# A fused retention and two-MoE-layer kernel: raw weights staged up to four tiles ahead, sixteen weight splits moved from VectorE to GpSimd, and half sums held in four buffers

## The chip, the cores and the metric

The kernel runs on one core of one Trainium2 chip. The metric is the device time of one execution in microseconds (us), lower is better. The core's engines are TensorE (PE in the rows, with its weight loads as PEld), VectorE (DVE), ScalarE (ACT), GpSimd (POOL) and SyncE (SP). Every transfer in this kernel is issued by SyncE's queue, in the order in which the program records it.

## The reference, cut to what matters

```python
# attention without softmax: B=4, H=8, S=768, D=64, one decay gamma per head
state = gamma * state + k[t] (x) v[t];   y[t] = scale * q[t] @ state
x = y as 3072 tokens x 512
# first layer, d_ff = 2048
h = x @ w_in;  g = h * sigmoid(1.702 * h);  x = g @ w_out
# second layer, d_ff = 1536
out = (sigmoid(x @ w_gate) * (x @ w_val)) @ w_out
```

All inputs are float32 except that the weights of both layers come to the kernel as 64-bit words (the bit patterns of doubles), which it converts itself.

## The kernel before, in words

**Arithmetic.** Each float32 operand of a large matmul is split into a rounded high part and a remainder (`wh`, `wl` for weights, `xh`, `xl` for tokens, `gh`, `gl` for the activation), and each product is three matmuls: high by high, high by low, low by high. ScalarE makes the high part, and VectorE or GpSimd subtracts to get the low part (`split_w`, lines 262 to 267, for a 128x512 weight tile).

**First phase, up to about 735 us of the profile.** The tokens are six blocks of 512 (`b` from 0 to 5), the first layer's inner dimension is sixteen slices of 128 (`f`). One pair `(b, f)` is a unit, 96 in all. A unit projects (`proj`, lines 270 to 275, twelve matmuls into a bank `h`), applies the gate (ScalarE L279, VectorE L280, ScalarE L283, VectorE L288), and two units later adds its output product (`emit_out`, lines 364 to 366, twelve matmuls into the four banks `acc`). The units run in segments: slices 0 to 7 of block 0, slices 0 to 7 of block 1, slices 8 to 15 of block 0, slices 8 to 15 of block 1, then blocks 2 to 5 with all sixteen slices each. So units 0 to 7 are the first segment, 8 to 15 the second, 16 to 23 the third, 24 to 31 the fourth. At the end of a segment `emit_out` moves the four banks to SBUF (tiles `ost`, two buffers) and stores them: as half sums to a DRAM tensor `halfd` after the first two segments, as the finished block to `x2d` after the others. In the third and fourth segment the half sums come back (`load_half`, three tiles at the segment's start and the fourth at its end) and are added.

Attention for the next block is cut into pieces (scores, state update, result) and one or two pieces are recorded with each unit. Their inputs `in_t` come through SyncE's queue into six buffers (`load_next`).

**Weights.** 68 tiles have to be converted: first 32 of the first layer, whose result stays in SBUF as `wraw`, then 36 of the second, whose result goes to a DRAM tensor `w2d`. `stage` (lines 202 to 208) issues the load of a raw tile (512 KB) into one of four buffers `w64` (named `w` in the rows). `convert` (lines 210 to 260) returns four steps that the unit's code calls at different points: a scaling on ScalarE (L228), two bit operations on VectorE (L233, L236), two more (L242, L246), and the sum (L256), on GpSimd for the first layer and on VectorE for the second, where the store to `w2d` (L258) follows. The last reader of a raw buffer is L246. Each of units 0 to 7 converts two tiles, units 8 to 20 one tile each, which ends the first layer's, and then five units of each eight convert a second-layer tile. The staging before keeps two raw tiles (units 0 to 6) or one (later) loaded ahead.

**What orders the work.** The schedule is manual: each engine runs its instructions in the order in which the loop over the units records them, and waits at the head of its queue. In a unit the order is: scaling and upper bits of this unit's conversion; the twelve `proj` matmuls; the split of the next unit's projection weight (`split_for`); the gate; the split of an output weight (`split_out`, always on GpSimd); lower bits; an attention piece; `gl`; the conversion's sum (and store); `stage`; perhaps a second attention piece; the output product of two units ago.

```python
            conv[3]()
            stage((2 if i < FH - 1 else 1) - len(staged))
            if items and b < 2:
                items.popleft()()
            pend.append(i)
            while pend and i - pend[0] >= DEPTH:
                emit_out(pend.popleft())
```

**Second phase, from about 735 us to the end.** The second layer runs as 36 chains of block products (lines 748 to 791). The change touches no line of it.

Of the kernel before, what the change touches and what calls it, by code (L numbers as in the profile page):

```python
# [8 lines left out]
F32 = mybir.dt.float32  # L9
# [6 lines left out]
P = 128  # L16
# [8 lines left out]
def retention_moe_moe2(  # L25
# [12 lines left out]
    nc = tc.nc  # L38
# [12 lines left out]
    def pool(stack, name, bufs, side, **kw):  # L51
        return stack.enter_context(tc.tile_pool(name=name, bufs=bufs, side=side, reuse_waits="tile", **kw))
# [5 lines left out]
    g_p = pool(left, "g", 2, "left")  # L58
# [3 lines left out]
    in_p = pool(right, "inp", 6, "right")  # L62
# [6 lines left out]
    def psum_tile(kind, shape=(P, 512)):  # L69
        i = turn[kind][0]  # L70
        turn[kind].rotate(-1)
        return psum[i].tile(list(shape), F32, name=kind, tag="bank")
# [11 lines left out]
    halfd = [dram.tile([P, KC, 512], F32, name=f"half{i}") for i in range(2)]  # L84
# [109 lines left out]
    raw1 = {}  # L194
    staged = deque()
# [6 lines left out]
    def stage(n=1):  # L202

        for _ in range(min(n, len(to_stage))):
            ph, f, k = to_stage.popleft()
            t = cv_p.tile([P, 512], U64, name="w64", tag="w64", bufs=4)
            nc.sync.dma_start(out=t, in_=(w1 if ph == "1" else w2)[f, k])
            staged.append((ph, f, k, t))
# [53 lines left out]
    def split_w(raw, lo_engine):  # L262
        wh = wsp_p.tile([P, 512], F32R, name="wh", tag="wh")
        wl = wsp_p.tile([P, 512], F32R, name="wl", tag="wl")
        nc.scalar.copy(wh, raw)  # L265
        lo_engine.tensor_tensor(out=wl, in0=raw, in1=wh, op=ALU.subtract)  # L266
        return wh, wl
# [22 lines left out]
    x_t, w_t, g_t, acc_t, half_t = {}, {}, {}, {}, {}  # L290
# [4 lines left out]
    def att_items(j):  # L295

        t0, n = blocks1[j]
        items = []
        for i in range(n // C):
            s = t0 // C + i  # L300

            def first(s=s, i=i):
                if i == 0:
                    alloc_x(j)
                emit_scores(s)
                if s >= 3:
                    load_next(s + 1, KN, V)

            def second(s=s):
                emit_update(s)  # L310
                if s >= 3:
                    load_next(s + 2, Q, K)

            def third(s=s, i=i):
                if s + 1 < NSTEP:
                    emit_prep(s + 1)
                emit_y(s, *x_t[j], i * C)

            items += [first, second, third]
        return deque(items)  # L320
# [3 lines left out]
    FH = F1 // 2  # L324
# [7 lines left out]
    def split_out(i):  # L332

        j = i - DEPTH
        if 0 <= j < len(units):
            w_t[j, "out"] = split_w(raw1[units[j][1], 1], nc.gpsimd)

    def split_for(i):

        if i < len(units):  # L340
            b, f = units[i]
            w_t[i, 0] = split_w(raw1[f, 0], nc.gpsimd if i < FH else nc.vector)

    def load_half(b):
        t = in_p.tile([P, 512], F32, name="half", tag="half", bufs=3)
        nc.sync.dma_start(out=t, in_=halfd[b][:, len(half_t[b]), :])
        half_t[b].append(t)

    def emit_out(i):
        b, f = units[i]  # L350
        if (b, f) in starts:
            acc_t[b] = [psum_tile("acc") for _ in range(4)]
            if f:
                half_t[b] = []
                for _ in range(3):
                    load_half(b)
        acc = acc_t[b]
        _, gh, gl = g_t.pop(i)
        wh, wl = w_t.pop((i, "out"))
        n = blocks1[b][1]  # L360
        st, sp = (b, f) in starts, (b, f) in ends
        for c in range(4):
            a, wc = acc[c][:, :n], slice(c * P, (c + 1) * P)
            nc.tensor.matmul(a, wh[:, wc], gh[:, :n], start=st, stop=False)  # L364
            nc.tensor.matmul(a, wl[:, wc], gh[:, :n], start=False, stop=False)  # L365
            nc.tensor.matmul(a, wh[:, wc], gl[:, :n], start=False, stop=sp)  # L366
        if not sp:
            return
        for c in range(4):
            t = g_p.tile([P, 512], F32, name="ost", tag="ost")  # L370
            if b in half_t:
                nc.vector.tensor_tensor(out=t, in0=acc[c], in1=half_t[b][c], op=ALU.add)
                if c == 0:
                    load_half(b)
            elif c % 2:
                nc.scalar.copy(t, acc[c])
            else:
                nc.vector.tensor_copy(t, acc[c])  # L378
            nc.sync.dma_start(out=(x2d if f == F1 - 1 else halfd)[b][:, c, :], in_=t)
# [20 lines left out]
    def open_early():  # L400
        p2["x"] = pool(ctx, "x2", 1, "right")
        p2["xt"] = pool(ctx, "xt", 6, "right")
        p2["w"] = [pool(ctx, "we", 1, "right")]
# [13 lines left out]
    def prep_x(g):  # L417

        hl = [
            [p2["x"].tile([P, 2, 512], F32R, name=f"{n}{j}", tag=f"{n}{j}") for n in ("xoh", "xol")] for j in range(7)  # L420
        ]
        xo[g] = hl
        for k in range(2):
            raw = {}
            for j, half, kk in ((B11, 0, k), (B12, 1, k), (B22, 1, k + 2), (B21, 0, k + 2)):
                raw[j] = p2["xt"].tile([P, 512], F32, name="xt", tag="xt")
                nc.sync.dma_start(out=raw[j], in_=x2d[2 * g + half][:, kk, :])
            yield
            for j in (T1, T2):
                raw[j] = p2["xt"].tile([P, 512], F32, name="xt", tag="xt")  # L430

            def diff(j, a, b):
                nc.gpsimd.tensor_tensor(out=raw[j], in0=raw[a], in1=raw[b], op=ALU.subtract)

            def split(j, engine):
                h, l = hl[j]
                nc.scalar.copy(h[:, k, :], raw[j])
                engine.tensor_tensor(out=l[:, k, :], in0=raw[j], in1=h[:, k, :], op=ALU.subtract)

            diff(T1, B12, B11)  # L440
            split(B11, nc.vector)
            yield
            diff(T2, B22, T1)
            split(B21, nc.vector)
            yield
            raw[T3] = raw[B12]
            diff(T3, B12, B22)
            split(T2, nc.vector)
            yield
            raw[T4] = raw[B21]  # L450
            diff(T4, B21, T2)
            split(T1, nc.vector)
            yield
            split(T3, nc.vector)
            yield
            split(T4, nc.gpsimd)
            split(B22, nc.vector)
            yield
# [174 lines left out]
    with tc.manual_schedule():  # L633
# [54 lines left out]
        for i, (b, f) in enumerate(units):  # L688
            if i == 0:
                items = att_items(1)  # L690
            elif (b, f) == (1, FH):
                items = att_items(2)
            elif b > 1 and f == 0:
                items = att_items(b + 1) if b + 1 < len(blocks1) else deque()
                if b == len(blocks1) - 1:
                    assert not staged and not to_stage
                    right.close()
                    open_early()
                    xs = prep_x(0)
                    load_chain(0)  # L700
            first = staged and staged[0][0] == "1"
            conv = [lambda: None] * 4
            if first:
                conv = convert(2 if i < FH else 1, nc.gpsimd)
            elif staged and (5 * i) // 8 > (5 * (i - 1)) // 8:
                conv = convert(1, nc.vector)
            xh, xl = x_t[b]
            n = blocks1[b][1]
            conv[0]()
            conv[1]()  # L710
            hb = psum_tile("h")
            proj(hb, w_t.pop((i, 0)), xh, xl, n)
            if i > 0:
                split_for(i + 1)
            g_t[i] = gated(hb, n)
            split_out(i + 1)
            conv[2]()
            if items and (b < 2 or f >= 1):
                items.popleft()()
            gated_lo(g_t[i], n)  # L720
            conv[3]()
            stage((2 if i < FH - 1 else 1) - len(staged))
            if items and b < 2:
                items.popleft()()
            pend.append(i)
            while pend and i - pend[0] >= DEPTH:
                emit_out(pend.popleft())
            next(xs, None)
            if b == len(blocks1) - 1:
                if f == 9:  # L730
                    sums(0)
                elif f in (11, 13):
                    split_chain(0, f == 13)()
# [141 lines left out]
```

## Time and profile before

| | |
|---|---|
| time, median of 3 runs | 1310.52 us (1307.9 to 1313.17) |
| the profiled execution's own time | 1308.13 us |
| its span | 1306.3 us |
| TensorE busy | 1218.8 us, 93% of the span |
| VectorE busy | 802.1 us, 61% |
| ScalarE busy | 546.3 us, 42% |
| GpSimd busy | 523.5 us, 40% |
| mean granted TensorE clock | 0.982 |

About 1.8 us of the profiled execution's time lie outside the span. Busy times are unions of an engine's instructions. A TensorE record covers a matmul from start to its modelled end, so records overlap: the distance between two starts tells the pace, and idle time counts from the end of the last record.

### The profile page before, as it was taken

What the parts mean: (1) busy time and instruction counts of PE and PEld (TensorE: products, weight loads), DVE (VectorE), ACT (ScalarE), POOL (GpSimd) and SP (SyncE); (2) the same over time, 40 slices, a digit from 0 to 9 for tenths busy, and PEclk for the clock granted to TensorE, in tenths of its full rate; (3) what the DMA queues carried; (4) which work ended last, traced back from release to release, by engine and by line L of the source; (5) the groups of instructions that cost most, each with busy time, mean ns of one, the idle gap of its engine ahead of it and who ended that gap; (6) DMA issues with size and microseconds to landing.
All of it is one profiled execution on the core that took longest, in us unless ns stands there. A gap on an engine that the chain in (4) does not pass through costs nothing.

```text
span 1306.3 us, 16095 instructions
## 1 busy us (share of the span) xinstructions
PE 1218.8 (93%) x5948; PEld 964.9 (74%) x5948; DVE 802.1 (61%) x1073; ACT 546.3 (42%) x964; POOL 523.5 (40%) x390
## 2 busy tenths in 40 slices
PE   7887998998999999989999899999899999899998
PEld 6665766776777777768788678787778777687877
DVE  5988986665666665756577263646554555635454
ACT  5333443343433443434455343435444344535251
POOL 4775442422231322322246362525652535643330
PEclk8889999999999999999999999999999999999999
DMA  8452322534224332332200220203321214211111
GB/s 283 162 192 83 127 105 78 189 109 158 91 103 135 108 127 83 129 105 74 93 28 1 98 80 25 73 25 107 119 73 34 64 44 126 97 57 49 49 33 65
DMA packets 62430, 123.48 MB, mean 95 GB/s; under 512 B 6800, under 2 KB 16016, under 8 KB 62352
## 3 DMA queue, kind: packets, MB, share of 16 engines
q1 hardware_dynamic: 62352, 122.46, 28.6%
q8 instruction: 47, 0.77, 0.3%
q14 instruction: 31, 0.25, 0.1%
HBM read 98.31 MB, written 24.12 MB: 94 GB/s over the span
## 4 chain that ended last, share of the span: by engine, by line
PE 51%; DVE 15%; DMA 9%; issue 8%; ACT 5%; POOL 3%; SPq 1%; ACTq 0%; POOLq 0%; DVEq 0%
PE pa L498 14%; DMA w<-in_w_dram 7%; PE pd L498 5%; PE po L616 4%; PE po L615 4%; PE po L614 4%; PE h L275 3%; PE pb L498 3%; PE h L273 3%; PE h L274 3%; PE acc L364 2%; PE acc L365 2%; PE acc L366 2%; DVE cva L256 2%; DVE sg L280 2%
## 5 line engine op out<-in xcount | busy, mean ns | idle before, releaser
L266 POOL TENSOR_TENSOR wl<-wraw,wh 128x512 fp32r<-128x512 f32 x104 | 150.7, 1449 | 428.8 <-ACT wh L265 401.6
L273 PE MATMUL h<-xh,wh 128*128 128x512 f32 x384 | 157.1, 409 | 26.8 <-ACT wh L265 19.1
L275 PE MATMUL h<-xh,wl 128*128 128x512 f32 x384 | 157.6, 410 | 10.4 <-DVE wl L266 9.3
L365 PE MATMUL acc<-gh,wl 128*128 128x512 f32 x384 | 153.5, 400 | 8.9 <-POOL wl L266 8.9
L364 PE MATMUL acc<-gh,wh 128*128 128x512 f32 x384 | 156.6, 408 | 3.6 <-DVE ost L378 2.8
L274 PE MATMUL h<-xl,wh 128*128 128x512 f32 x384 | 155.1, 404 | 0.2 <-DVE xl L190 0.2
L366 PE MATMUL acc<-gl,wh 128*128 128x512 f32 x384 | 150.5, 392 | 0.0
L498 PE MATMUL pa<-xoh,oh 128*128 128x512 f32 x288 | 115.1, 400 | 16.4 <-ACT u L557 11.7
L490 POOL TENSOR_TENSOR ol<-raw,oh 128x768 fp32r<-128x768 f32 x36 | 66.8, 1857 | 153.1 <-ACT oh L487 152.9
L283 ACT CAST gh<-sg 128x512 fp32r<-128x512 f32 x96 | 59.6, 621 | 160.9 <-DVE sg L280 160.9
L233 DVE TENSOR_SCALAR cva<-cva 128x512 uint32<-128x512 uint32 x68 | 53.8, 795 | 115.0 <-ACT cva L228 114.0
L265 ACT CAST wh<-wraw 128x512 fp32r<-128x512 f32 x192 | 116.2, 613 | 0.2
L498 PE MATMUL pa<-xol,oh 128*128 128x512 f32 x288 | 114.4, 397 | 0.0
L498 PE MATMUL pa<-xoh,ol 128*128 128x512 f32 x288 | 113.3, 393 | 0.8 <-DVE ol L490 0.8
L614 PE MATMUL po<-woh,g2h 128*128 128x512 f32 x288 | 112.4, 390 | 1.1 <-DVE ost L507 1.1
L616 PE MATMUL po<-woh,g2l 128*128 128x512 f32 x288 | 112.5, 391 | 0.0
L615 PE MATMUL po<-wol,g2h 128*128 128x512 f32 x288 | 112.5, 391 | 0.0
L273 PEld LDWEIGHTS h<-xh,wh 128*128 128x128 f32 x384 | 74.6, 194 | 49.9 <-ACT wh L265 26.2
L228 ACT ACTIVATE cva<-w 128x512 f32<-128x512 f32 x68 | 45.4, 669 | 156.2 <-DMA w<-in_w_dram 142.7
L275 PEld LDWEIGHTS h<-xh,wl 128*128 128x128 f32 x384 | 74.6, 194 | 35.1 <-DVE wl L266 17.4
L365 PEld LDWEIGHTS acc<-gh,wl 128*128 128x128 f32 x384 | 72.5, 189 | 30.8 <-POOL wl L266 17.7
L364 PEld LDWEIGHTS acc<-gh,wh 128*128 128x128 f32 x384 | 72.4, 188 | 26.9 <-DVE ost L378 3.6
(108 smaller groups left out, 2521.7 us busy)
## 6 DMA issues: line engine op xcount, KB each, us to landing
w<-in_w_dram SPq DMA_DIRECT2D x68, 512.0 KB, 4.0
in_t<-in_qkv_dram SPq DMA_DIRECT2D x96, 256.0 KB, 3.5
raw<-w2d SPq DMA_DIRECT2D x72, 256.0 KB, 3.1
w2d<-cva SPq DMA_DIRECT2D x36, 256.0 KB, 2.2
wor<-w2d SPq DMA_DIRECT2D x36, 256.0 KB, 2.7
x2d<-ost SPq DMA_DIRECT2D x24, 256.0 KB, 2.9
xt<-x2d SPq DMA_DIRECT2D x24, 256.0 KB, 4.4
out_dram<-ost SPq DMA_DIRECT2D x24, 256.0 KB, 2.0
```

The lines of the kernel that those rows point to most:

```text
L265: nc.scalar.copy(wh, raw)
L266: lo_engine.tensor_tensor(out=wl, in0=raw, in1=wh, op=ALU.subtract)
L273: nc.tensor.matmul(bank[:, :n], wh[:, k, :], xh[:, k, :n], start=(k == 0), stop=False)
L274: nc.tensor.matmul(bank[:, :n], wh[:, k, :], xl[:, k, :n], start=False, stop=False)
L275: nc.tensor.matmul(bank[:, :n], wl[:, k, :], xh[:, k, :n], start=False, stop=(k == KC - 1))
L364: nc.tensor.matmul(a, wh[:, wc], gh[:, :n], start=st, stop=False)
L365: nc.tensor.matmul(a, wl[:, wc], gh[:, :n], start=False, stop=False)
L366: nc.tensor.matmul(a, wh[:, wc], gl[:, :n], start=False, stop=sp)
L498: nc.tensor.matmul(bank, w[:, kk], x[:, k, :], start=start and k == 0 and w is wh and x is xh, stop=stop and k == 1 and w is wl, skip_grou ...
L614: nc.tensor.matmul(bank, gh, wh, start=f == 0, stop=False)
L615: nc.tensor.matmul(bank, gh, wl, start=False, stop=False)
L616: nc.tensor.matmul(bank, gl, wh, start=False, stop=f == FR - 1)
```

## The change

Three things are changed in the first phase. `stage` is called so that four raw tiles are loaded or on their way after each unit, with the same four buffers. The low part of the projection weight's split is computed by GpSimd for units 0 to 23, where it was GpSimd for units 0 to 7 and VectorE from unit 8. And for blocks 0 and 1 the four output tiles of a segment's end are four different buffers (three tiles `half` and one `ost`), the half sums are reloaded into the same four at the segment's start, and the sum is written in place. Blocks 2 to 5 use `ost` with two buffers as they did.

```diff
-            w_t[i, 0] = split_w(raw1[f, 0], nc.gpsimd if i < FH else nc.vector)
-
-    def load_half(b):
-        t = in_p.tile([P, 512], F32, name="half", tag="half", bufs=3)
-        nc.sync.dma_start(out=t, in_=halfd[b][:, len(half_t[b]), :])
-        half_t[b].append(t)
+            w_t[i, 0] = split_w(raw1[f, 0], nc.gpsimd if i < 3 * FH else nc.vector)
+
+    def half_tile(c):
+        if c < 3:
+            return in_p.tile([P, 512], F32, name="half", tag="half", bufs=3)
+        return g_p.tile([P, 512], F32, name="ost", tag="ost")
 
     def emit_out(i):
         b, f = units[i]
...
             if f:
                 half_t[b] = []
-                for _ in range(3):
-                    load_half(b)
+                for c in range(4):
+                    half_t[b].append(half_tile(c))
+                    nc.sync.dma_start(out=half_t[b][c], in_=halfd[b][:, c, :])
...
         for c in range(4):
-            t = g_p.tile([P, 512], F32, name="ost", tag="ost")
+            t = half_t[b][c] if b in half_t else half_tile(c) if b < 2 else half_tile(3)
             if b in half_t:
                 nc.vector.tensor_tensor(out=t, in0=acc[c], in1=half_t[b][c], op=ALU.add)
-                if c == 0:
-                    load_half(b)
...
             conv[3]()
-            stage((2 if i < FH - 1 else 1) - len(staged))
+            stage(4 - len(staged))
```

The queue of SyncE where the first second-layer tiles are stored (units 18 to 24; `w_` with a number is one raw tile's buffer as the program names it, so the numbers differ between the programs). Before:

```order
L207 DMA w_1673<-in_w_dram 128x512
L346 DMA half<-half_128 128x512 x3
L207 DMA w_1734<-in_w_dram 128x512
L207 DMA w_1785<-in_w_dram 128x512
L258 DMA w2d<-cva 128x512
L207 DMA w_1836<-in_w_dram 128x512
L258 DMA w2d<-cva 128x512
L207 DMA w_1927<-in_w_dram 128x512
```

Of the change:

```order
L207 DMA w_1679<-in_w_dram 128x512
L357 DMA half<-half_128 128x512 x3
L357 DMA ost<-half_128 128x512
L207 DMA w_1742<-in_w_dram 128x512
L207 DMA w_1793<-in_w_dram 128x512
L258 DMA w2d<-cva 128x512
L207 DMA w_1844<-in_w_dram 128x512
L258 DMA w2d<-cva 128x512
L207 DMA w_1935<-in_w_dram 128x512
```

The pattern is the same, one load behind each store, but the loads are of later tiles. Before, 33 raw tiles stand ahead of the first store, and that store is of the 33rd tile, so the load behind it is of the very next tile to be converted. Now 36 stand ahead of it, and the load behind it is of the tile that is converted fourth from there.

GpSimd's queue in units 7 to 9 (`wl` is a weight's low part, `wraw` a converted first-layer tile). Before:

```order
L266 TENSOR_TENSOR wl<-wraw,wh 128x512
L256 TENSOR_TENSOR wraw<-cva,cvb 128x512 x2
L266 TENSOR_TENSOR wl<-wraw,wh 128x512
L256 TENSOR_TENSOR wraw<-cva,cvb 128x512
L266 TENSOR_TENSOR wl<-wraw,wh 128x512
```

Of the change:

```order
L266 TENSOR_TENSOR wl<-wraw,wh 128x512 x2
L256 TENSOR_TENSOR wraw<-cva,cvb 128x512 x2
L266 TENSOR_TENSOR wl<-wraw,wh 128x512 x2
L256 TENSOR_TENSOR wraw<-cva,cvb 128x512
L266 TENSOR_TENSOR wl<-wraw,wh 128x512 x2
```

A unit had one split and one or two sums on GpSimd, and now has two splits beside them; VectorE's queue has one L266 fewer in each of these units.

## Rows read from the trace of the kernel before

**Rows 1.** Windows: length, busy PE, PEld, DVE, ACT, POOL, granted clock, DMA share, GB/s.

```profile
30.00:112.00 82.00, 64.93 (x391) 50.09 (x387) 74.82 (x99) 34.07 (x63) 55.53 (x37) 0.92 0.48 156
112.00:205.00 93.00, 85.11 (x343) 62.76 (x344) 82.06 (x104) 40.89 (x73) 44.29 (x30) 1.00 0.29 99
205.00:330.00 125.00, 112.69 (x663) 88.67 (x662) 80.50 (x121) 46.89 (x88) 34.20 (x24) 0.97 0.43 138
330.00:640.00 310.00, 289.11 (x1570) 225.84 (x1569) 195.72 (x290) 124.71 (x229) 84.21 (x61) 0.98 0.32 107
```

**Rows 2.** TensorE's waits, 330 to 640 us: total us, times, longest.

```profile
PE h L273 <- ACT wh L265: 13.6, 9, 2.5
PE h L275 <- DVE wl L266: 5.5, 10, 0.6
PE acc L365 <- POOL wl L266: 1.7, 3, 0.6
```

**Rows 3.** TensorE's waits, 205 to 330 us.

```profile
PE h L273 <- ACT wh L265: 5.4, 2, 2.8
PE h L273 <- DVE sg L280: 3.5, 1, 3.5
```

**Rows 4.** Timeline of all engines, around unit 53: start, duration, idle before and releaser.

```profile
439.08 0.33 SPq L258 DMA_DIRECT2D w2d<-cva  x1
...
439.46 0.42 SPq L207 DMA_DIRECT2D w<-in_w_dram  x1
...
443.25 0.66 ACT L228 ACTIVATE cva<-w 128x512 f32<-128x512 f32 x1 [6.72 <-DMA w<-in_w_dram]
...
443.94 0.43 DVE L233 TENSOR_SCALAR cva<-cva 128x512 uint32<-128x512 uint32 x1 [4.89 <-ACT cva L228]
...
444.40 0.69 DVE L236 SCALAR_TENSOR_TENSOR cva<-w,cva 128x512 uint32<-128x512 uint32 x1
```

**Rows 5.** Timeline of TensorE around 410 us.

```profile
409.53 0.39 PE L273 MATMUL h<-xh,wh 128*128 128x512 f32 x1
409.76 0.39 PE L274 MATMUL h<-xl,wh 128*128 128x512 f32 x1
...
410.37 0.63 PE L273 MATMUL h<-xh,wh 128*128 128x512 f32 x1
```

**Rows 6.** Timeline of VectorE, one unit of the second segment.

```profile
145.12 1.31 DVE L233 TENSOR_SCALAR cva<-cva 128x512 uint32<-128x512 uint32 x1
146.47 1.66 DVE L236 SCALAR_TENSOR_TENSOR cva<-w,cva 128x512 uint32<-128x512 uint32 x1
148.05 0.68 DVE L266 TENSOR_TENSOR wl<-wraw,wh 128x512 fp32r<-128x512 f32 x1
148.65 0.68 DVE L280 TENSOR_TENSOR sg<-h,sg 128x512 f32<-128x512 f32 x1
...
151.11 1.31 DVE L233 TENSOR_SCALAR cva<-cva 128x512 uint32<-128x512 uint32 x1
```

**Rows 7.** Timeline of GpSimd, the same unit.

```profile
144.59 1.56 POOL L266 TENSOR_TENSOR wl<-wraw,wh 128x512 fp32r<-128x512 f32 x1 [3.00 <-ACT wh L265]
146.11 1.47 POOL L256 TENSOR_TENSOR wraw<-cva,cvb 128x512 f32<-128x512 f32 x1
```

**Rows 8.** Timeline of ScalarE around the second segment's end.

```profile
169.90 0.60 ACT L279 ACTIVATE sg<-h 128x512 f32<-128x512 f32 x1 [0.31 <-PE h L275]
...
178.88 0.59 ACT L376 COPY ost<-acc 128x512 f32<-128x512 f32 x1 [3.90 <-DMA half<-ost]
...
190.98 0.60 ACT L279 ACTIVATE sg<-h 128x512 f32<-128x512 f32 x1 [0.31 <-PE h L275]
```

**Rows 9.** Waits of ScalarE, VectorE and SyncE's queue, 30 to 112 us.

```profile
ACT cva L228 <- DMA w<-in_w_dram: 8.7, 5, 2.8
...
DVE cva L233 <- ACT cva L228: 6.8, 8, 1.9
...
SPq L207 <- DVE cvb L246: 23.0, 3, 7.8
```

## The prediction

> **What bounds the kernel now.** I read the first phase by stages [rows 1], since the change touches nothing behind about 735 us. VectorE is the fullest engine up to 205 us: it is busy 74.82 of 82 us from 30 to 112 us and 82.06 of 93 us from 112 to 205 us. From 205 us on it falls to 80.50 of 125 and 195.72 of 310 us, and TensorE is the bound, but with holes: it is idle 125 - 112.69 = 12.3 us there and 310 - 289.11 = 20.9 us behind. So three stages have three different limits, and each part of the change falls in another.
>
> What makes the holes behind 330 us is read from TensorE's waits: 13.6 us for ScalarE's `wh`, 5.5 us for VectorE's `wl` right behind it, 1.7 us for GpSimd's `wl` [rows 2]. These add up to 20.8 of the 20.9 us. Unit 53 shows what ScalarE itself was late for [rows 4]. The queue of SyncE takes the store of a converted tile at 439.08 us, when VectorE's sum is done, and only then the load behind it, at 439.46 us. The tile of that load is the one ScalarE wants next, and L228 starts at 443.25 us after 6.72 us of waiting. The cast of the next unit's weight stands behind L228 on ScalarE, so TensorE, which has two units of work in hand, runs dry soon after. This hurts where two units in a row convert, which the rule of five in eight makes happen twice in eight units: the load has one unit's time minus the conversion's own length, and a lone conversion has two.
>
> **Part 1, raw tiles four ahead.** In the queue of the change the load behind a store is of the tile that is converted fourth from there, at least six units later, against a load that needs about 4 us (439.46 to 443.25) [rows 4]. So these waits should all go. The load has to wait for the last reader L246 of its own buffer, but the store ahead of it waits for the sum L256, which comes after L246, so behind 205 us nothing new is waited for.
>
> The sum for 205 to 640 us: idle time that hangs on these waits is 20.8 us [rows 2] and 5.4 + 3.5 = 8.9 us [rows 3] (the 3.5 us stand behind a VectorE that waited for the same load), together 29.7 us in 9 + 10 + 3 + 2 + 1 = 25 holes. A record lasts 0.39 us while the next start normally follows after 0.23 [rows 5], so each hole hides 0.16 us more: 4 us. Third, the clock. Around 410 us, after a hole, a record of the same matmul is 0.63 us long instead of 0.39 [rows 5], which is 0.24 us more, as much again as the pace of 0.23: the lower of the two levels (1.2 instead of 2.4 GHz). The granted clock of 0.98 over 310 us and 0.97 over 125 us [rows 1] lacks at most 0.02 x 310 + 0.03 x 125 = 10 us of full pace, part of it inside the holes; I take 6 us. Sum 29.7 + 4 + 6 = 40 us. I keep 3 us back for holes that another engine opens once this one is closed, since VectorE's busy share will rise from 63% to about 70% there: **37 us**, between 20 (half of it lost again) and 40.
>
> From 30 to 112 us ScalarE waits 8.7 us for raw tiles, and VectorE, the bound there, waits 6.8 us in all for ScalarE's L228 [rows 9]. Not all of these eight waits follow a late load (ScalarE has other reasons to be late with L228, a scaling buffer above all), and the change leaves those. The gain is between 0 and 6.8 us; I take the middle: **3 us**.
>
> **Part 2, sixteen splits to GpSimd.** This falls in units 8 to 23, where VectorE repeats a tight loop of 151.11 - 145.12 = 6.0 us [rows 6], while 24 matmuls at 0.23 us want 5.5. The removed L266 costs 0.60 us of the loop (148.05 to 148.65), which alone would bring 6.0 to 5.4 and leave TensorE as the bound: 14 units x 0.5 = 7 us gained. But the loop shows a price for GpSimd's work. L233 takes 1.31 and L236 1.66 us beside GpSimd's two operations [rows 6, 7], and 0.43 and 0.69 us in a place where GpSimd is idle [rows 4]: 1.85 us lost to two operations, so 0.93 each. A third operation on GpSimd in every unit would, at the same price, cost 0.93 and bring 0.60: the loop becomes 6.3, and 14 x 0.33 = 5 us are lost. What decides is whether the third one lies beside L280, which keeps its 0.68 us when it reads the bank in PSUM, or beside the SBUF operations. GpSimd would be busy some 4.5 of 6 us, too much to miss them all. I take **0 us**, between 7 gained and 5 lost.
>
> The Trainium skill has a rule that speaks against this part (SBUF — State Buffer, "Who interferes with whom"): VectorE instructions with two SBUF inputs or in a two-port mode and GpSimd instructions share a port pair that one holds for its whole instruction while the other is blocked. The slow L233 and L236 agree with it, and so does L280. Were no overlap at all possible, the loop would be GpSimd's three operations plus VectorE's own SBUF work, which the rival below prices; the row of 6.0 us is shorter than the same reckoning for two operations (3.0 + 3.5 = 6.5), so the trace bears it out only in part.
>
> **Part 3, four buffers for half sums.** At the second segment's end ScalarE waits 3.90 us until a store has landed and frees an `ost` buffer, and three units take 190.98 - 169.90 = 21.1 us instead of 18.0 [rows 8]: 3.1 us. With four buffers the four evictions need no store. The moves themselves stay (two on VectorE, about 1.2 us of a full loop, are in the 3.1 and don't go). So some 2 us at each of the first two ends: **4 us**. The ends of the third and fourth segment lie behind 205 us, where TensorE has slack for them; I count nothing for them. Reloading the halves all at the start puts one more transfer into SyncE's queue eight units ahead of its use.
>
> **The sum.** 37 + 3 + 0 + 4 = 44 us off the profiled execution's 1308.1 us, which lies 2.4 us under the median of the runs: about **1265 us**.
>
> **The rivals.** (a) *Another engine takes the place of the load.* With L228 on time, VectorE in two converting units in a row has its conversion twice beside an attention piece, and a late L266 stops TensorE as a late `wh` did. Against it: 63% busy from 330 to 640 us [rows 1], and TensorE's slack of two units. It would halve part 1, 37 / 2 = 18: 1265 + 18 = 1283 us. (b) *GpSimd blocks VectorE in units 8 to 23.* With no overlap the loop is three GpSimd operations (4.5 us) plus VectorE's SBUF work free of disturbance, which is the loop less the loss, L266 and L280 (6.0 - 1.85 - 0.60 - 0.68 = 2.9 us): 7.4 us, which is 14 x 1.4 = 20 us lost: 1285 us. For it: L236 at 1.66 us. Against it: the reckoning that is too long for the loop of before. (c) *Slower than before: the loads stop SyncE's queue in the first segment.* In units 0 to 6 a load now has to wait for L246 of its own unit at the head of the queue, and attention's `in_t` stand behind it. Such waits are there already, 23.0 us in three places, longest 7.8 [rows 9]. If each of 7 units stopped TensorE's attention for 7.8 us, 55 us would be lost against 41 gained elsewhere: 1322 us. It decides from about 6 us per unit; but `in_t` is loaded a step or more ahead, and the queue already spends such time waiting without TensorE waiting for a transfer. (d) *More than forecast:* the loop of units 8 to 23 falls to TensorE's pace and the first segment gains its 6 us: 1265 - 10 = 1255 us or a little less.
>
> **How the numbers follow.** My forecast has 0.70, (a) 0.12, (b) 0.08, (c) 0.03, (d) 0.07. A measurement of this kernel tells 0.5% (6.5 us) from no change. All but (c) are well under 1304 us; for losses of which I know nothing I give 0.03 to "same". So faster 0.94, same 0.03, slower 0.03. The forecast's own range is 1255 to 1277 us; for 8 in 10 with parts of (a), (b) and (d) I give 1250 to 1284.
>
> **What the changed kernel's profile would show.** Part 1 right: behind 205 us ScalarE's wait for raw tiles is gone or a few us, TensorE has almost no wait for `wh`, its idle time falls to about 5 us, and the granted clock is 1.00 there; the first phase ends some 44 us earlier. Wrong, if TensorE waits for VectorE's `wl` or `sg` instead. Part 2: the distance of two L233 in units 11 to 17, 5.5 to 6.3 us; more than 6.5 says (b). Part 3: no wait of L376 for a store of `half`. Part (c) would show as TensorE or GpSimd waiting for `in_t` before 112 us. The second phase should last as long as before; if it doesn't, the prediction is off for a reason not considered here.

## The result and the profile after

The changed kernel takes 1253.53 us (median of 4 runs, 1252.34 to 1254.23) against 1311.85 us for the kernel before (4 runs): a ratio of 0.9553, 95% interval 0.952 to 0.9587, or 58 us less. The prediction said 1265 us with a range of 1250 to 1284, so the direction and the mechanism held. The time is inside that range, but 1.5 us under the forecast's own range of 1255 to 1277, and the gain was a third larger than the 44 us of its sum.

The windows of the changed kernel over the first phase, in the columns of [rows 1], with ends moved to its own units:

```profile
30.00:112.00 82.00, 65.30 (x385) 50.66 (x386) 77.27 (x96) 33.18 (x61) 60.21 (x39) 0.91 0.51 167
112.00:204.00 92.00, 86.59 (x359) 66.81 (x358) 88.73 (x91) 42.32 (x78) 68.14 (x45) 0.99 0.37 118
204.00:330.00 126.00, 126.00 (x800) 101.79 (x798) 98.80 (x141) 55.01 (x103) 41.05 (x28) 1.00 0.46 151
330.00:581.00 251.00, 251.00 (x1405) 202.60 (x1402) 189.76 (x263) 112.31 (x206) 77.54 (x54) 1.00 0.36 115
```

From 204 to 581 us TensorE is busy for 126.00 of 126 and 251.00 of 251 us at a granted clock of 1.00, where before it idled 33 us and the clock was 0.97 and 0.98 [rows 1]. All waits of TensorE in that stretch that [rows 2, 3] list are gone. ScalarE's longest waits from 330 to 581 us (total, times, longest) hold no raw tile any more:

```profile
ACT sg L279 <- PE h L275: 94.7, 34, 3.8
ACT gh L283 <- DVE sg L280: 33.9, 39, 1.5
ACT ost L375 <- DMA x2d<-ost: 8.0, 2, 4.1
```

ScalarE now waits for TensorE's projections, which is what an engine beside the bound should do. The timeline of ScalarE around unit 53, where [rows 4] had it waiting 6.72 us:

```profile
400.96 0.62 ACT L283 CAST gh<-sg 128x512 fp32r<-128x512 f32 x1 [0.76 <-DVE sg L280]
401.49 0.62 ACT L265 CAST wh<-wraw 128x512 fp32r<-128x512 f32 x1
402.01 0.67 ACT L228 ACTIVATE cva<-w 128x512 f32<-128x512 f32 x1
402.58 0.60 ACT L265 CAST wh<-wraw 128x512 fp32r<-128x512 f32 x1
406.37 0.60 ACT L279 ACTIVATE sg<-h 128x512 f32<-128x512 f32 x1 [3.18 <-PE h L275]
```

L228 stands there with no wait in front of it, and the cast of the next unit's weight is done 3.2 us before ScalarE can go on at all.

Where the time came from is read from the start of L279, one in each unit, in ScalarE's timeline of each kernel (us):

| unit | before | changed | gained so far | what lies in between |
|---|---|---|---|---|
| 8 | 110.90 | 108.69 | 2.2 | first segment |
| 17 | 169.90 | 166.73 | 3.2 | loop, first segment end |
| 23 | 209.86 | 203.90 | 6.0 | loop, second segment end |
| 32 | 285.90 | 268.54 | 17.4 | first second-layer conversions |
| 80 | 637.28 | 581.22 | 56.1 | conversions to their end |
| 95 | 720.84 | 664.76 | 56.1 | no conversion |

The second phase is as long as it was: 1306.3 - 720.84 = 585.5 us before and 1251.2 - 664.76 = 586.4 us now.

### The profile page after: what moved, and what is told of

The parts are those of the page before. It is cut to its first block, busy times and chain, and to the rows that moved or that the text cites. A ratio compares the mean times of both kernels' runs of the same rounds, so it can differ in the third digit from the quotient of the medians.

```text
span 1251.2 us, 16113 instructions
## 1 busy us (share of the span) xinstructions
PE 1196.4 (96%) x5948; PEld 959.4 (77%) x5948; DVE 826.2 (66%) x1057; ACT 545.8 (44%) x964; POOL 552.2 (44%) x406
## 4 chain that ended last, share of the span: by engine, by line
PE 69%; issue 7%; POOL 7%; DVE 5%; ACT 3%; DMA 1%; SPq 0%; POOLq 0%; DVEq 0%; ACTq 0%
PE pa L497 15%; PE acc L365 5%; PE pd L497 5%; PE acc L366 5%; PE acc L367 5%; PE h L275 5%; PE h L274 5%; PE h L273 5%; PE po L615 4%; PE po L614 4%; PE po L613 4%; POOL wl L266 3%; PE pb L497 3%; POOL wraw L256 2%; DVE g2l L527 1%
## 5 line engine op out<-in xcount | busy, mean ns | idle before, releaser
L266 POOL TENSOR_TENSOR wl<-wraw,wh 128x512 fp32r<-128x512 f32 x120 | 176.4, 1471 | 345.4 <-ACT wh L265 324.6
L275 PE MATMUL h<-xh,wl 128*128 128x512 f32 x384 | 152.6, 397 | 2.7 <-POOL wl L266 2.6
L273 PE MATMUL h<-xh,wh 128*128 128x512 f32 x384 | 152.2, 396 | 2.8 <-DVE xl L190 1.1
L274 PE MATMUL h<-xl,wh 128*128 128x512 f32 x384 | 151.9, 396 | 0.2 <-DVE xl L190 0.2
L279 ACT ACTIVATE sg<-h 128x512 f32<-128x512 f32 x96 | 57.4, 598 | 189.3 <-PE h L275 189.2
L497 PE MATMUL pa<-xoh,oh 128*128 128x512 f32 x288 | 115.7, 402 | 16.6 <-ACT u L556 11.7
L280 DVE TENSOR_TENSOR sg<-h,sg 128x512 f32<-128x512 f32 x96 | 65.9, 686 | 55.8 <-ACT sg L279 55.8
L288 DVE TENSOR_TENSOR gl<-sg,gh 128x512 fp32r<-128x512 f32 x96 | 82.6, 860 | 17.2 <-ACT gh L283 17.2
```

What stands on the lines that cost most here:

```text
L273: nc.tensor.matmul(bank[:, :n], wh[:, k, :], xh[:, k, :n], start=(k == 0), stop=False)
L274: nc.tensor.matmul(bank[:, :n], wh[:, k, :], xl[:, k, :n], start=False, stop=False)
L275: nc.tensor.matmul(bank[:, :n], wl[:, k, :], xh[:, k, :n], start=False, stop=(k == KC - 1))
L497: nc.tensor.matmul(bank, w[:, kk], x[:, k, :], start=start and k == 0 and w is wh and x is xh, stop=stop and k == 1 and w is wl, skip_grou ...
```

## The experiments

**Four ahead alone.** The kernel before with one line changed:

```diff
-            stage((2 if i < FH - 1 else 1) - len(staged))
+            stage(4 - len(staged))
```

> The kernel before with only the staging changed to four tiles ahead. My theory (a raw load stands in the transfer queue behind the store of the tile before, so it comes too late for the next conversion, and this alone is what the changed kernel gains behind 205 us): nearly all of the gain, 50 us behind the third segment and about 2 us ahead of it, so 1258 us (1254 to 1264), with no wait of TensorE for a weight's high part from 330 us to the first phase's end. The rival (the gain comes from the work taken off VectorE and from the buffers of the half sums, the loads being only the last of several waits): less than half of it, 1285 us or more.

Measured: 1258.69 us, ratio 0.9601 (0.957 to 0.9632), 52 us less. The window from 204 to 640 us, in the columns of [rows 1]:

```profile
204.00:640.00 436.00, 433.54 (x2440) 349.03 (x2439) 325.94 (x446) 195.60 (x359) 141.26 (x98) 1.00 0.37 117
```

TensorE's waits there come to 2.3 us in four holes (33.2 us of idle time before). The rival is out: the staging alone is most of the gain, and the load was the wait that ended last.

**The splits alone.** The kernel before with

```diff
-            w_t[i, 0] = split_w(raw1[f, 0], nc.gpsimd if i < FH else nc.vector)
+            w_t[i, 0] = split_w(raw1[f, 0], nc.gpsimd if i < 3 * FH else nc.vector)
```

> The kernel before with only the sixteen splits moved to GpSimd. My theory (a GpSimd operation that lies beside VectorE's SBUF work costs VectorE about 0.9 us, more than the 0.6 us that the removed split frees): the loop of units 11 to 17 goes from 6.0 to 6.1 or 6.3 us, and the time is 1 to 4 us longer than before, ratio 1.001 to 1.003. The rival (VectorE is relieved): the loop falls to 5.5 us and the time by 5 to 7 us, ratio 0.995.

Measured: 1313.1 us, ratio 1.0014 (0.9997 to 1.0032). The time by itself can't tell 2 us from none. The loop can: from unit 11 to 17 a unit takes 6.21 us, against 5.99 before, and unit 23 starts its gate 1.7 us later (211.51 against 209.86). Two units of VectorE in this run:

```profile
139.62 1.28 DVE L233 TENSOR_SCALAR cva<-cva 128x512 uint32<-128x512 uint32 x1
140.94 1.66 DVE L236 SCALAR_TENSOR_TENSOR cva<-w,cva 128x512 uint32<-128x512 uint32 x1
142.53 0.68 DVE L280 TENSOR_TENSOR sg<-h,sg 128x512 f32<-128x512 f32 x1
143.13 0.91 DVE L242 TENSOR_SCALAR cvb<-cva 128x512 uint32<-128x512 uint32 x1
144.07 0.69 DVE L246 SCALAR_TENSOR_TENSOR cvb<-w,cvb 128x512 f32<-128x512 uint32 x1
144.68 1.78 DVE L288 TENSOR_TENSOR gl<-sg,gh 128x512 fp32r<-128x512 f32 x1
146.39 1.52 DVE L233 TENSOR_SCALAR cva<-cva 128x512 uint32<-128x512 uint32 x1
147.94 1.66 DVE L236 SCALAR_TENSOR_TENSOR cva<-w,cva 128x512 uint32<-128x512 uint32 x1
149.53 0.68 DVE L280 TENSOR_TENSOR sg<-h,sg 128x512 f32<-128x512 f32 x1
150.13 0.41 DVE L242 TENSOR_SCALAR cvb<-cva 128x512 uint32<-128x512 uint32 x1
150.57 0.69 DVE L246 SCALAR_TENSOR_TENSOR cvb<-w,cvb 128x512 f32<-128x512 uint32 x1
151.18 0.68 DVE L288 TENSOR_TENSOR gl<-sg,gh 128x512 fp32r<-128x512 f32 x1
151.98 1.29 DVE L233 TENSOR_SCALAR cva<-cva 128x512 uint32<-128x512 uint32 x1
```

The units alternate. One takes 146.39 - 139.62 = 6.8 us, with L242 (0.91) and L288 (1.78) slowed beside L233 and L236; the next takes 151.98 - 146.39 = 5.6 us, where both have their free 0.41 and 0.68 us. L280, which reads PSUM, has 0.68 in both. Over the two units the added contention is 0.50 (L242), 1.10 (L288) and 0.24 (the longer L233, 1.52), together 1.84 us, or 0.92 for each operation added.

**The four buffers alone.** The changed kernel with the other two edits taken back, so that of the diff only `half_tile` and its uses remain:

```diff
-            w_t[i, 0] = split_w(raw1[f, 0], nc.gpsimd if i < 3 * FH else nc.vector)
+            w_t[i, 0] = split_w(raw1[f, 0], nc.gpsimd if i < FH else nc.vector)
...
-            stage(4 - len(staged))
+            stage((2 if i < FH - 1 else 1) - len(staged))
```

> The kernel before with only the four buffers for half sums. My theory: the store waits at the ends of the first and second segment go, 2 to 3 us each, and one hole at the end of the third and fourth segment each of about 1 us; 5 to 7 us less than before, ratio 0.995. The rival (the ends are hidden under the units in hand, since TensorE is idle for only 2.8 us there): 0 to 2 us less, ratio 0.999.

Measured: 1300.21 us, ratio 0.9918 (0.9888 to 0.9948), 11 us less. More than my theory said, and the rival is out. By the starts of L279 this run is ahead of the kernel before by 5.7 us at unit 23, 8.9 at unit 28 and 11.7 at unit 95. The next experiment shows where the gain lies once the loads are on time.

**The change without the splits.** The changed kernel with

```diff
-            w_t[i, 0] = split_w(raw1[f, 0], nc.gpsimd if i < 3 * FH else nc.vector)
+            w_t[i, 0] = split_w(raw1[f, 0], nc.gpsimd if i < FH else nc.vector)
```

> The changed kernel with the sixteen splits back on VectorE. My theory (the move costs VectorE more than it frees): 2 us less than the changed kernel, 1251 us (1248 to 1253), with a loop of 6.0 us in units 11 to 17 against 6.2 on average in the changed kernel. The rival (with raw tiles on time the move relieves VectorE): 2 to 6 us more than the changed kernel, 1256 to 1260 us.

Measured: 1249.23 us, ratio 0.9526 (0.9498 to 0.9554), 4 us less than the changed kernel; the intervals of the two ratios overlap, so the times alone don't separate them. In the traces the loop is 6.02 us against 6.20 from unit 11 to 17. The changed kernel is 0.5 us ahead at unit 8, 2.6 us behind at unit 9, 3.1 at unit 17 and 4.2 at unit 23 (203.90 against 199.69), and stays 4.2 us behind to unit 95 (664.76 against 660.53). So moving the splits cost 4 us: about 2 in the loop, 0.2 us in each unit, and the rest at the start of the second segment.

Set beside four ahead alone, this run also prices the buffers: 1258.69 - 1249.23 = 9.5 us. The second segment's end, ScalarE's timeline, first with four ahead alone, then with the buffers too:

```profile
168.11 0.60 ACT L279 ACTIVATE sg<-h 128x512 f32<-128x512 f32 x1 [0.32 <-PE h L275]
...
178.10 0.59 ACT L376 COPY ost<-acc 128x512 f32<-128x512 f32 x1 [4.91 <-DMA half<-ost]
...
184.12 0.60 ACT L279 ACTIVATE sg<-h 128x512 f32<-128x512 f32 x1 [0.22 <-PE h L275]
```

```profile
163.62 0.60 ACT L279 ACTIVATE sg<-h 128x512 f32<-128x512 f32 x1 [0.32 <-PE h L275]
...
168.61 0.59 ACT L375 COPY ost<-acc 128x512 f32<-128x512 f32 x1
...
175.62 0.60 ACT L279 ACTIVATE sg<-h 128x512 f32<-128x512 f32 x1 [0.21 <-PE h L275]
```

Two units take 16.0 us with the store wait and 12.0 us without it, which is exactly two of the loop's 6.0: nothing of the eviction is left. The lead of this run over four ahead alone is 4.5 us at unit 17, 8.5 at 23, 10.5 at 28 and 11.5 at 36 and at 95, so the first two ends gave about 4.5 and 4 us and the third and fourth another 2 and 1.

**Two ahead instead of four.** The kernel before with

```diff
-            stage((2 if i < FH - 1 else 1) - len(staged))
+            stage(2 - len(staged))
```

> The kernel before with the staging kept at two tiles throughout (it was two in units 0 to 6 and one later). My theory (what matters is that the load of the next tile no longer stands behind the store of the one before it; how deep is of no account): as with four ahead, 1259 us (1255 to 1264), and no wait of ScalarE for a raw tile above 1 us behind 205 us. The rival (the depth of four is needed, because one conversion more of lead is still shorter than queue and load together): half of it, 1280 us or more, with waits of ScalarE for raw tiles where two units in a row convert.

Measured: 1260.62 us, ratio 0.961 (0.959 to 0.963). From 204 to 640 us ScalarE has no wait for a raw tile among its waits:

```profile
ACT sg L279 <- PE h L275: 154.5, 59, 4.6
ACT gh L283 <- DVE sg L280: 73.3, 67, 5.7
ACT ost L376 <- DMA x2d<-ost: 11.9, 3, 4.3
```

Four is not needed; two do the same.

**One ahead, but the load in front of the store.** The kernel before with

```diff
-            conv[3]()
             stage((2 if i < FH - 1 else 1) - len(staged))
+            conv[3]()
```

> The kernel before with the staging as deep as it was, but the load recorded ahead of the conversion's sum and store instead of behind them. My theory (the lateness is the place in the transfer queue, not the number of tiles): nearly all of the gain of four ahead, 1260 us (1256 to 1268). The rival (one tile ahead is too few wherever the load stands, since its 4 us and the queue in front of it take up the unit): less than half of it, 1285 us or more.

Measured: 1259.7 us, ratio 0.9609 (0.9585 to 0.9633). The cause is the place in the queue: with no tile more ahead than before and the same buffers, the same 52 us are gained. The lead is thinner, though. SyncE's queue in this run (a store, inputs of attention, a load), and ScalarE's wait from 330 to 587 us:

```profile
398.91 0.33 SPq L258 DMA_DIRECT2D w2d<-cva  x1
399.67 7.14 SPq L93 DMA_DIRECT2D in_t<-in_qkv_dram  x2
406.87 0.42 SPq L207 DMA_DIRECT2D w<-in_w_dram  x1
410.45 0.33 SPq L258 DMA_DIRECT2D w2d<-cva  x1
```

```profile
ACT cva L228 <- DMA w<-in_w_dram: 35.2, 11, 3.9
```

The load now goes out 3.6 us before the unit's own store, held by attention's inputs instead, and ScalarE still waits 35.2 us in 11 places. None of these waits is over 3.9 us, and TensorE's two units of work in hand cover them: its waits from 204 to 640 us come to 1.8 us. In the kernel before, the same waits from 330 to 640 us were longer, and not all of them were covered [rows 2]:

```profile
ACT cva L228 <- DMA w<-in_w_dram: 94.3, 22, 7.2
```

**Sums on VectorE.** From the change without the splits:

```diff
-                conv = convert(2 if i < FH else 1, nc.gpsimd)
+                conv = convert(2, nc.gpsimd) if i < FH else convert(1, nc.vector)
```

> Four ahead and four buffers, the splits on VectorE from unit 8 as before, and also the conversion sums of units 8 to 20 moved from GpSimd to VectorE. My theory (a GpSimd operation beside VectorE's SBUF work costs VectorE 0.9 us, doing it itself costs 0.6): the loop of units 11 to 17 falls from 6.0 to 5.7 us or less and the time by 3 to 5 us against the version without the move of splits, 1245 us (1242 to 1248). The rival (VectorE is full there, so every operation more on it lengthens the loop): the loop rises to 6.6 us and the time to 1257 us.

Measured: 1245.99 us, ratio 0.9503 (0.9489 to 0.9517), 3 us under the change without the splits, with ratio intervals that overlap. The loop of units 11 to 17 tells more: it falls from 6.02 to 5.61 us although VectorE has an operation more in it. At unit 95 this run is 1.9 us ahead (658.66 against 660.53). VectorE and then GpSimd in one such unit:

```profile
144.40 1.79 DVE L256 TENSOR_TENSOR wraw<-cva,cvb 128x512 f32<-128x512 f32 x1
146.12 0.41 DVE L233 TENSOR_SCALAR cva<-cva 128x512 uint32<-128x512 uint32 x1
146.56 0.69 DVE L236 SCALAR_TENSOR_TENSOR cva<-w,cva 128x512 uint32<-128x512 uint32 x1
147.17 0.68 DVE L266 TENSOR_TENSOR wl<-wraw,wh 128x512 fp32r<-128x512 f32 x1
```

```profile
144.07 1.57 POOL L266 TENSOR_TENSOR wl<-wraw,wh 128x512 fp32r<-128x512 f32 x1 [4.07 <-ACT wh L265]
149.72 1.56 POOL L266 TENSOR_TENSOR wl<-wraw,wh 128x512 fp32r<-128x512 f32 x1 [4.07 <-ACT wh L265]
```

GpSimd has one operation per unit, and one operation of VectorE pays for it: L256 takes 1.79 us beside it. L233 and L236, which took 1.31 and 1.66 us in [rows 6], have 0.41 and 0.69 us now that GpSimd is idle beside them. Where GpSimd is idle L256 takes 0.68 us (in 11 places of the trace of before), so the price of a GpSimd operation is 1.79 - 0.68 = 1.1 us here, more than the 0.93 of the prediction.

The rows also show what sets this price. L256 ends at 144.40 + 1.79 = 146.19 us, 0.55 us behind the end of GpSimd's L266 (144.07 + 1.57 = 145.64). In [rows 6, 7] L236 ends 0.55 us behind GpSimd's L256 in the same way, and L233 0.28 us behind L266. In all ten traces, up to unit 95, every lengthened operation of these lines on 128x512 tiles ends so: those with two SBUF operands (L236, L246, L256, L266, L288) 0.54 to 0.56 us behind the end of a GpSimd operation, L233 and L242 0.28 to 0.29 us. So VectorE's operation, where it is held, waits until GpSimd's ends, and the price is what is left of GpSimd's operation when VectorE's begins, not a fixed 0.93 or 1.1 us.

**In the first segment too.** From the run with the sums on VectorE:

```diff
-            w_t[i, 0] = split_w(raw1[f, 0], nc.gpsimd if i < FH else nc.vector)
+            w_t[i, 0] = split_w(raw1[f, 0], nc.vector)
...
-                conv = convert(2, nc.gpsimd) if i < FH else convert(1, nc.vector)
+                conv = convert(2 if i < FH else 1, nc.vector)
```

> As the run with the sums of units 8 to 20 on VectorE, and in units 0 to 7 as well: both conversion sums and the projection split on VectorE, so that GpSimd keeps only the output splits and attention's two operations. My theory (the same price): two sums and one split per unit, each 0.3 us cheaper on VectorE, and the scaling on ScalarE no longer waits for GpSimd to free its buffer; about 6 us less than with the sums of units 8 to 20 alone, 1239 us (1234 to 1244). The rival (in the first segment VectorE's own work is the bound and GpSimd has the room): 5 us or more longer than that, 1250 us or more.

Measured: 1240.6 us, ratio 0.9461 (0.9443 to 0.9479), the shortest of all and 13 us under the changed kernel. Unit 7 starts its gate at 96.57 us against 102.59 in the run before it. Two things changed at once here and no run separates them: VectorE has fewer GpSimd operations beside it, and ScalarE's waits with L228 for the sum L256 to free a scaling buffer fall from 19.2 to 14.2 us. Of the 6.0 us only 1.0 is left at unit 8 (107.41 against 108.36), and 4.8 at unit 95. In between, GpSimd was held up:

```profile
93.63 6.03 POOL L266 TENSOR_TENSOR wl<-wraw,wh 128x512 fp32r<-128x512 f32 x1 [5.48 <-ACT wh L265]
```

From 93.63 to 98.46 us VectorE ran operations on SBUF back to back at their free lengths, until its L280, which reads PSUM, began. GpSimd's operation ended 1.2 us behind that, at 99.66, and TensorE waited 4.9 us for its `wl`. So the hold also works the other way: here a full VectorE delayed a split left on GpSimd.

## Why the prediction was right, and where its sizes were off

**What bounds the kernel** was read rightly. The loads behind the stores were the cause (one ahead in front of the store gives the same 52 us), and TensorE's full pace was what stood behind them. One reading of [rows 1] was wrong: from 112 to 205 us VectorE was not the fullest engine, since TensorE was busy 85.11 of 93 us and VectorE 82.06. VectorE's loop was the limit all the same, as its fall to 5.61 us with the sums on VectorE shows.

**Part 1, the largest error.** The term for 205 to 640 us was 37 us, between 20 and 40. Four ahead alone brought 427.4 us from unit 23 to unit 80 (209.86 to 637.28) down to 380.3 (208.21 to 588.52): 47 us, outside that bound. The mis-sized steps are "each hole hides 0.16 us more" with the terms beside it, and the 3 us held back. The run with only the four buffers still has holes and shows two of them whole:

```profile
342.39 0.50 PE L273 MATMUL h<-xh,wh 128*128 128x512 f32 x1 [2.39 <-ACT wh L265]
342.73 0.39 PE L274 MATMUL h<-xl,wh 128*128 128x512 f32 x1
343.67 0.51 PE L275 MATMUL h<-xh,wl 128*128 128x512 f32 x1 [0.55 <-DVE wl L266]
344.02 0.40 PE L273 MATMUL h<-xh,wh 128*128 128x512 f32 x1
344.25 0.40 PE L274 MATMUL h<-xl,wh 128*128 128x512 f32 x1
```

The first matmul behind a hole has a record of 0.50 us, and the next starts 0.34 us after it instead of 0.23. So a hole costs 0.11 us behind it besides the 0.16 us in front. The distances between the starts of all matmuls of the units from 23 to 80 in the trace of before, less the usual pace, add up so: 28 holes, 36 us with the part in front of them (I had 29.7 + 4, having left out the small holes that rows 2 and 3 don't show); about 3 us behind them (I had nothing); 8 us of matmuls at the slower pace (I had 6). A 29th hole, in front of attention's scores, is there with four ahead as well. The 3 us held back for holes that another engine would open were not needed: none opened. That makes the 47.

**Its first-segment term**, 3 us, came to 1.7 us by unit 23 with four ahead alone. The waits of L228 for raw tiles did go, 8.7 us of them [rows 9], but its waits for GpSimd to free a scaling buffer grew from 13.5 to 19.2 us. ScalarE's wait from 30 to 112 us, before and in the run with four ahead alone:

```profile
ACT cva L228 <- POOL wraw L256: 13.5, 5, 4.9
ACT cva L228 <- POOL wraw L256: 19.2, 7, 4.9
```

**Part 2** was put at 0 between 7 gained and 5 lost, and cost 4 us. The price per operation was right in kind (a free L266 of 0.60 us on VectorE was bought at 0.92 us of contention in the loop), and a loop of 6.2 us lies inside "5.5 to 6.3". I took the middle where the row spoke for the loss: with GpSimd busy 4.5 us of 6, a third operation couldn't find a free place in every unit, and finds one in every second.

**Part 3** was put at 4 us and gave 10. Two steps failed: that 1.2 us of moves stay (two units take 12.0 us, the loop's own time), and that the third and fourth ends are hidden by TensorE's slack (3 us of the 11.5 in the trace lie there; with four ahead alone TensorE's scores still wait 1.5 us for VectorE's `xl` near the third end, and in the changed kernel they don't; where the other 1.5 us come from stays open). The first two ends were also under-sized, 2 us each against 4.5 and 4.

**The rivals.** (a) another engine takes over: no, TensorE has no wait from 204 to 581 us. (b) GpSimd blocks VectorE without overlap, a loop of 7.4 us: no, 6.2 us. The mechanism is there, since each slowed operation is held until GpSimd's ends, but adding up whole lengths over-prices it: only what is left of an operation is waited for, and L280 runs beside GpSimd unhindered. (c) the loads stop the queue in the first segment: the queue of the changed kernel waits there for L246 much more than before [rows 9], and nothing comes of it:

```profile
SPq L207 <- DVE cvb L246: 46.1, 16, 9.7
```

TensorE, ScalarE and GpSimd show no wait for `in_t` from 30 to 112 us; the inputs have the lead that the prediction gave them. (d) more than forecast: the time came near it, 1253.5 against 1255 us, but not by its mechanism; the loop didn't reach TensorE's pace, and the surplus is that of parts 1 and 3. The range held for a reason it was not made for.

## What to carry to other kernels

In a transfer queue that runs in order, look at what stands in front of a load, not only at how many are kept ahead: a load recorded behind a store that waits for computed data can't start before that data is done, and either moving it ahead of the store or one tile more of lead took TensorE's waits for it away here. When holes in TensorE are to be closed, count their number beside their idle time, since here each hole cost about 0.27 us more than its idle time, and slower matmuls on top. And before work is moved from a full VectorE to an idle GpSimd, weigh what it frees against what the GpSimd operation costs its neighbours: with 0.6 us freed and 0.9 to 1.1 us paid, moving the conversion sums the other way was the gain.

## What the runs showed of the hardware

A GpSimd operation of about 1.5 us on 128x512 makes a neighbour on VectorE longer when that one reads two SBUF operands (0.68 or 0.69 us free, up to 1.66 to 1.79 beside GpSimd) or is one of the two `uint32` operations on SBUF, L233 and L242 (0.41 us free, 1.3 and 0.91 us in the rows above). The neighbour ends a fixed 0.55 or 0.28 us behind the end of GpSimd's operation. L280, with one operand in PSUM, kept its 0.68 us throughout. The rule of the Trainium skill that the prediction cites (SBUF — State Buffer, "Who interferes with whom") names the same operations as sharing a port pair with GpSimd, and these rows agree. I hadn't expected the cost of a third operation per unit to alternate: in one unit it fell on VectorE's L242 and L288, in the next on nothing, so the loop swung between 6.8 and 5.6 us, in the changed kernel too, and its mean of 6.2 hides both.
